# Attention, Fourier mixing and two feed-forward layers in one kernel: inputs handed over in the order of use, half the features in the first Fourier contraction, five probability buffers

## The chip, the core and the metric

The kernel runs on one core of a Trainium2 chip. TensorE (PE) multiplies matrices and transposes, VectorE (DVE) and ScalarE (ACT) do elementwise work, GpSimd (POOL) does elementwise work on SBUF alone and issues some DMAs, and SyncE (SP) issues most DMAs. Each engine takes its instructions in the order in which the program was written for it. PE writes to PSUM only, and DVE or ACT must carry its results on. The metric is the device time of one execution in microseconds (us); lower is better. What the host does with the inputs ahead of the launch is not in that time.

## The reference, cut to what matters

```python
# q, k, v: (4 batches, 8 heads, 576 rows, 64), float32
scores = (q @ k.T) / 8
scores = where(scores >= max(scores) - tau, scores, -1e9)
attn   = softmax(scores) @ v
x   = concat of the heads              # (4, 576, 512)
u   = x + real(fft(fft(x, axis=1), axis=2))
un  = (u - mean) / sqrt(var + 1e-6)    # over the 512 features
y   = u + relu(un @ w_ch1) @ w_ch2     # 512 -> 2048 -> 512
gate = sigmoid(causal 5-tap convolution of y over the rows, per feature)
out = (gate * (y @ w_val)) @ w_out
```

The weights come as float64 and are converted on the chip. Everything is kept at float32 accuracy: a matrix product with a weight or a Fourier table is three products of "high" and "low" parts (names end in h and l).

## The kernel before

The program has three stages, which follow one another on PE.

**Attention and Fourier mixing** (function attention_fft). The work goes by 16 pairs of heads, four pairs a batch. A pair has nine score tiles of 128 queries; two tiles make a unit, so there are 72 units. What each engine gets in a unit, and in which order, stands in one string (ORDER, line 34): each word is one step, T for the transposes of the probabilities of two units ago, S for the next scores, M, TH, E, K for maximum, threshold, exponential and masking, N for the division by the row sums. In order of data: PE makes scores s (line 582); DVE takes the maximum neg (594) and the threshold thr (597); ACT makes e (601); DVE masks into p and sums (611); POOL divides p by the sum (618); PE turns p into t (652); ACT copies it to m (661); PE multiplies m with v (318). The score tiles have two PSUM buffers, so the scores of the next unit wait until DVE has masked the tile before (line 611).

Between those fixed steps PE gets *filler* work in two places of each unit (P1 and P2, budgets of 1250 and 1350 ns), taken from queues in the order of QORD: the transposes of the last 64 keys (632), the preparation of the next pair's q and k, the Fourier products, the products with v. Steps on POOL, SP and ACT that belong to fillers run as *side* generators, advanced twice in a unit (A1, A2).

- Preparation of q and k (g_prep_qk, 247): natural q and k tiles are loaded in 128-partition pieces of 64 floats a row (load_qk, 179), q twice. PE turns them (258, 268, 277: 14 transposes a pair), DVE copies the keys out of PSUM (264, 272), ACT copies the queries and scales them by alpha = 1/8 (271, 279).
- Fold (g_fold, 331): a pair's x is stored to a DRAM tile xs; POOL makes sums and differences of row n and row 576-n (346, 348), ACT their high part (351), POOL the low part (355). All four pairs of a batch go into the contraction.
- Fourier products (g_fft, 376): stage one contracts the 512 features (four blocks of 128) with cosines and sines: 6 output blocks of 12 products, 72 a batch (line 398, recorded at 242). Stage two contracts rows: 45 products a batch (421). Features 257 to 511 are the mirror of 1 to 255, so the second half is fetched in reversed order (xr); the reversal goes through DRAM in two DMAs (turn_blocks 368, turn_order 372), and again for the result (472 to 481).

While this runs, weight pieces (40 in all) are loaded by POOL, converted on DVE, ACT and POOL (lines 96 to 106) in slots of the same units, and the first 18 are stored to DRAM and fetched back when room in SBUF comes free.

**Feed-forward** (mlp). Five chunks of columns; per chunk 16 steps of 12 products h (1083) and 12 products c (1099). Chunk 0 is interleaved with the last batch's Fourier products (line 1275), the rest follow.

**Gate and output** (gate_out): convolution on DVE, products v (1396) and o (1414).

## Time and profile before

| | |
|---|---|
| runs of the kernel before | 919.17 us median of 3 (919.12 to 919.69) |
| the profiled execution | 920.12 us, its span 918.3 us |
| PE busy | 874.0 us, 95% of the span |
| DVE, ACT, POOL busy | 558.9, 452.6, 370.1 us |
| granted PE clock, mean | 0.998 |
| DMA | 127.03 MB in 135019 packets, 87454 of them under 512 B |

A busy share is the union of an engine's instruction times. PE's matmuls overlap, so the mean duration of one (0.28 us for a transpose) is longer than the time from one to the next; for the pace one takes a run of several. The shares are averages over stages with different limits, so they are read stage by stage below.

### The profile page before, as it was taken

To read this page: it belongs to the slowest core of one execution; us is meant where nothing else is said; L and a number is where in the kernel's file an instruction comes from. 1 tells how busy PE (TensorE), PEld (TensorE's weight loads), DVE (VectorE), ACT (ScalarE), POOL (GpSimd) and SP (SyncE) were. 2 spreads that over 40 slices of the span, in tenths; PEclk is the share of its full clock that TensorE was granted. 3 is DMA by queue.
4 is the path that set the end of the run, shared out by engine and by line. 5 is a ranking of instruction groups with operands and counts; after the bars stand their busy time and mean duration, and the time that the engine had idled before them with its cause. 6 is when DMAs were issued, how large, how long until landed. Compare 5 with 4: busy or idle time off the path is not lost.

```text
span 918.3 us, 14887 instructions
## 1 busy us (share of the span) xinstructions
PE 874.0 (95%) x5232; PEld 693.7 (76%) x5232; DVE 558.9 (61%) x1240; ACT 452.6 (49%) x915; POOL 370.1 (40%) x451
## 2 busy tenths in 40 slices
PE   5988899999899999999999999999999999999998
PEld 3555576656656676578878999999888888898896
DVE  6888888888887676625885445434122375626740
ACT  4787777777776766735553333223112122214432
POOL 2465654675467427624563232221110201047421
PEclk9999999999999999999999999999999999999999
DMA  6776565567556622599259541421200230154101
GB/s 152 197 182 149 162 185 161 162 198 195 165 172 204 155 90 65 156 331 351 93 163 340 211 168 36 146 76 37 90 1 1 97 99 1 46 184 144 63 36 70
DMA packets 135019, 127.03 MB, mean 138 GB/s; under 512 B 87454, under 2 KB 93854, under 8 KB 134944
## 3 DMA queue, kind: packets, MB, share of 16 engines
q1 hardware_dynamic: 126496, 101.26, 36.0%
q0 software_dynamic: 6960, 24.49, 8.8%
q8 instruction: 42, 0.69, 0.3%
q10 hardware_dynamic: 1488, 0.33, 0.2%
q14 instruction: 33, 0.27, 0.1%
HBM read 93.53 MB, written 41.96 MB: 148 GB/s over the span
## 4 chain that ended last, share of the span: by engine, by line
PE 69%; DVE 12%; issue 9%; POOL 4%; ACT 4%; DMA 2%; SPq 0%; DVEq 0%; POOLq 0%; ACTq 0%
PE c L1099 16%; PE h L1083 16%; PE f L318 8%; PE s L582 7%; PE f L242 6%; PE o L1414 5%; PE v L1396 4%; PE t L652 4%; DVE p L611 4%; DVE neg L594 3%; ACT e L601 1%; PE f L632 1%; DVE ct L97 1%; POOL p L618 1%; PE f L277 1%
## 5 line engine op out<-in xcount | busy, mean ns | idle before, releaser
L1086 ACT ACTIVATE hh<-h 128x512 fp32r<-128x512 f32 (+1 forms) x80 | 44.3, 554 | 248.3 <-PE h L1083 248.2
L1087 DVE SCALAR_TENSOR_TENSOR hl<-h,hh 128x512 fp32r<-128x512 f32 (+1 forms) x80 | 50.8, 636 | 182.1 <-ACT hh L1086 182.1
L618 POOL TENSOR_SCALAR p<-p,su 128x576 f32<-128x576 f32 x144 | 110.6, 774 | 90.0 <-DVE su L708 70.8
L611 DVE SCALAR_TENSOR_TENSOR p<-s,thr,e 128x576 f32<-128x576 f32 x144 | 112.6, 815 | 39.9 <-ACT e L601 20.7
L582 PE MATMUL s<-kt,qt 64*128 64x288 f32 (+1 forms) x640 | 100.5, 445 | 24.7 <-DVE p L611 24.7
L1099 PE MATMUL c<-hl,w1h 128*128 128x512 f32 (+1 forms) x320 | 117.8, 368 | 0.4 <-DVE hl L1087 0.4
L1099 PE MATMUL c<-hh,w1h 128*128 128x512 f32 (+1 forms) x320 | 117.6, 367 | 0.0
L1099 PE MATMUL c<-hh,w1l 128*128 128x512 f32 (+1 forms) x320 | 117.5, 367 | 0.0
L594 DVE TENSOR_REDUCE neg<-s 128x1 f32<-128x576 f32 x144 | 101.5, 744 | 18.3 <-PE s L582 18.3
L601 ACT ACTIVATE e<-s,neg 128x576 f32<-128x576 f32 x144 | 99.5, 736 | 22.6 <-DVE neg L594 22.1
L582 PEld LDWEIGHTS s<-kt,qt 64*128 64x128 f32 (+1 forms) x640 | 45.7, 176 | 66.4 <-DVE p L611 22.8
L661 ACT ACTIVATE m<-t 128x512 f32<-128x512 f32 x144 | 84.6, 587 | 8.7 <-PE t L652 8.7
L318 PE MATMUL f<-m,v 128*64 128x320 f32 (+1 forms) x512 | 80.4, 415 | 1.6 <-ACT m L661 1.3
L652 PE MATMUL t<-ident,p 128*128 128x128 f32 x576 | 78.7, 279 | 2.3 <-POOL xf L346 1.2
L1083 PE MATMUL h<-unh,w0h 128*128 128x512 f32 (+1 forms) x320 | 79.1, 369 | 1.0 <-DMA w0h<-e_h 0.9
L1083 PE MATMUL h<-unh,w0l 128*128 128x512 f32 (+1 forms) x320 | 78.9, 368 | 0.1
L1083 PE MATMUL h<-unl,w0h 128*128 128x512 f32 (+1 forms) x320 | 78.7, 367 | 0.0
L652 PEld LDWEIGHTS t<-ident,p 128*128 128x128 f32 x576 | 64.2, 142 | 18.7 <-POOL p L618 8.4
L1099 PEld LDWEIGHTS c<-hl,w1h 128*128 128x128 f32 x320 | 60.1, 188 | 8.7 <-DVE hl L1087 1.2
L1083 PEld LDWEIGHTS h<-unh,w0h 128*128 128x128 f32 x320 | 58.5, 188 | 9.7 <-DMA w0h<-e_h 1.3
L1099 PEld LDWEIGHTS c<-hh,w1l 128*128 128x128 f32 x320 | 60.1, 188 | 7.2
L1099 PEld LDWEIGHTS c<-hh,w1h 128*128 128x128 f32 x320 | 60.1, 188 | 7.3
(219 smaller groups left out, 1543.5 us busy)
## 6 DMA issues: line engine op xcount, KB each, us to landing
raw<-in_moe_w_ch POOLq DMA_DIRECT2D x32, 512.0 KB, 5.0
qn<-in_q SPq DMA_DIRECT2D x60, 128.0 KB, 3.0
xs<-xt SPq DMA_DIRECT2D x16, 288.0 KB, 2.8
e_h<-cx SPq DMA_DIRECT2D x18, 256.0 KB, 4.4
e_l<-ct SPq DMA_DIRECT2D x18, 256.0 KB, 2.1
ypad<-y_d SPq DMA_DIRECT2D x16, 288.0 KB, 2.9
out<-os SPq DMA_DIRECT2D x18, 256.0 KB, 2.0
w0h<-e_h SPq DMA_DIRECT2D x17, 256.0 KB, 5.4
```

The costliest lines, as they stand in the source:

```text
L242: PE.matmul(out=o, lhsT=l, rhs=r, start=(i == 0), stop=(i == n - 1))
L318: PE.matmul(out=f[h * 64:h * 64 + 64, 0:n], lhsT=w, rhs=r, start=(t == 0), stop=(t == 4))
L582: PE.matmul(out=s[o, c, 0:HALF], lhsT=qt[w, hh, q], rhs=kt[w, hh, :], start=True, stop=True)
L594: DVE.tensor_reduce(out=neg[i][:, j, 0:1], in_=sc[g][:, :, 0:HALF], axis=AX.XY, op=ALU.max, negate=True)
L601: ACT.activation(e, sc[g][:, :, 0:HALF], AF.Exp, bias=neg[g // 2][:, g % 2, 0:1], scale=1.0)
L611: DVE.scalar_tensor_tensor(out=p_view(g).rearrange("p (a b) -> p a b", a=2), in0=sc.pop(g)[:, :, 0:HALF], scalar=thr[g // 2][:, j], in1=ex ...
L618: POOL.tensor_scalar(out=v, in0=v, scalar1=su, scalar2=1.0, op0=ALU.mult, op1=ALU.mult)
L652: PE.matmul(out=f[:, t, :], lhsT=pv[:, t * 128:(t + 1) * 128], rhs=ident, is_transpose=True, start=(t == 0), stop=(t == 3))
L661: tq.append(lambda: ACT.activation(o, fv, AF.Copy))
L1083: PE.matmul(out=f[:, 0:n], lhsT=ww[:, k * 128:(k + 1) * 128], rhs=x[:, k, 0:n], start=(i == 0), stop=(i == 3 * KB - 1))
L1087: DVE.scalar_tensor_tensor(out=hl, in0=f[:, 0:n], scalar=0.0, in1=f32(hh), op0=ALU.max, op1=ALU.subtract)
L1099: PE.matmul(out=ch[c][o][:, 0:n], lhsT=ww[:, o * 128:(o + 1) * 128], rhs=x, start=(at_ == 0 and i == 0), stop=(at_ == FB - 1 and i == 2))
```

## The change

The host now hands over q transposed (64 features by both heads' 576 rows), k transposed with its two halves on two sets of 64 partitions, v in tile order, all with the features of heads 4 to 7 mirrored, and the weights' rows and columns permuted to match. The kernel loads q and k where they are used; POOL scales k by alpha (DVE for the first pair). The pairs are taken in the order 2, 3, 0, 1: the upper two are only stored (reversed order comes by itself) and read back as *mirror*; for the lower two POOL adds and subtracts the mirror (1152 columns more) before the fold. Stage one contracts two feature blocks instead of four, plus one small product `od` that carries the alternating term of feature 256. The result's second half is stored without a reversal. PBUFS goes from 4 to 5. The marks that open room for the feed-forward stage are set by unit (LEFT = 100, in tiles), and the last chunk uses its weight slots from the highest down.

```diff
-PBUFS = 4
+PBUFS = 5
+WAIT_QK = 2
+LEFT = 100
-QORD = (1, 0, 4, 2, 3)
+QORD = (0, 3, 1, 2)
+PAIRS = (2, 3, 0, 1)
+TURN = (2, 2)
...
+            kt = qk_p.tile([128, 2, HALF], F32, tag="kt", name="kt")
+            qt = qk_p.tile([128, 2, S], F32, tag="qt", name="qt")
+            SP.dma_start(out=kt, in_=a["k"][b, n])
+            for j, q in enumerate((SP, second)):
+                q.dma_start(out=qt[j * 64:j * 64 + 64], in_=a["q"][b, n])
+            return qt, kt
+
+        def g_prep_qk(p):
+            qt, kt = load_qk(p)
+            for _ in range(WAIT_QK):
+                yield
+            POOL.tensor_scalar(out=kt, in0=kt, scalar1=alpha[:, 0:1], scalar2=1.0, op0=ALU.mult, op1=ALU.mult)
+            kq[p] = (qt, kt)
...
-                    PE.transpose(f[:, o:o + 128], kn[:, j, h].rearrange("p g d -> p (g d)"), ident)
...
-                done(lambda: None, lambda: DVE.tensor_copy(kt[:, :, 0:256], fk))
...
-                PE.transpose(f[:, h * 96:h * 96 + 96], tn[:, h].rearrange("p g d -> p (g d)"), ident[0:96, 0:96])
...
-                    PE.transpose(f[:, t * 128:(t + 1) * 128], qn[:, h, t].rearrange("p g d -> p (g d)"), ident)
...
-                done(lambda f=f, h=h: ACT.activation(qt[:, h, 0:MAIN], f, AF.Identity, scale=alpha[:, 0:1]))
...
+            if j >= 2:
+                r = 1 + 128 * (3 - j)
+                SP.dma_start(out=rev[r:r + 128], in_=x)
+                if j == 2:
+                    SP.dma_start(out=rev[0:1], in_=x[127:128])
+                folded.add(p)
+                if p % NP == 1:
+                    for _ in range(TURN[0]):
+                        yield
+                    while b and b - 1 not in spent_fold:
+                        yield
+                    ms = [fft_p.tile([128, S], F32, tag=f"mirror{i}", name="mirror") for i in range(2)]
+                    for i, m in enumerate(ms):
+                        SP.dma_start(out=m, in_=rev[i * 128:(i + 1) * 128])
...
+            eng = DVE if p == NPAIR - 1 else POOL
...
+            eng.tensor_tensor(out=d, in0=x, in1=m, op=ALU.subtract)
+            yield
+            eng.tensor_tensor(out=m, in0=x, in1=m, op=ALU.add)
+            yield
+            turn(1, d, ALU.subtract)
+            if j == 0:
+                POOL.tensor_tensor(out=t[1][0:1, inner], in0=d[0:1, inner], in1=d[0:1, back], op=ALU.add)
+            yield
+            turn(0, m, ALU.add)
+            high_part(1)
+            yield
+            low_part(1)
             high_part(0)
             yield
-            high_part(1)
             low_part(0)
...
-                    for xx, dd in ((xh, dh), (xl, dh), (xh, dl)):
-                        for j in range(NP):
-                            yield mm(f[0:m, 0:n], xx[:, j, n0:n0 + m], dd[:, j, 0:n], i, 12)
-                            i += 1
+                    terms = [(xx[:, j, n0:n0 + m], dd[:, j, 0:n]) for xx, dd in ((xh, dh), (xl, dh), (xh, dl)) for j in range(2)]
+                    if kind == 0:
+                        terms += [(xx[:, 0, n0:n0 + m], cst["od"]) for xx in fold[b][1]]
+                    for i, (xx, dd) in enumerate(terms):
+                        yield mm(f[0:m, 0:n], xx, dd, i, len(terms))
...
-            turn_blocks(blocks, rev, 16)
-            if j == 0:
-                SP.dma_start(out=u_d[b][256:257], in_=rev[0:1])
-            yield
-            turn_order(u_d[b][DM - 127 - 128 * j:DM + 1 - 128 * j], blocks, 16)
+            SP.dma_start(out=u_d[b][DM // 2 + 128 * j:DM // 2 + 128 * j + 128], in_=xr)
```

On PE, at the start of the program, before the change (kn, tn, qn are natural keys, tails and queries; s the scores):

```order
L258 MATMUL f<-ident,kn 128x128 x4
L268 MATMUL f<-ident,tn 128x96 x2
L277 MATMUL f<-ident,qn 128x128 x8
L582 MATMUL s<-kt,qt 128x288 x4
L258 MATMUL f<-ident,kn 128x128 x4
L268 MATMUL f<-ident,tn 128x96 x2
L582 MATMUL s<-kt,qt 128x288 x4
L277 MATMUL f<-ident,qn 128x128 x8
```

The same place after the change, down to the first products with v:

```order
L539 MATMUL s<-kt,qt 128x288 x12
L609 MATMUL t<-ident,p 128x128 x8
L539 MATMUL s<-kt,qt 128x288 x4
L609 MATMUL t<-ident,p 128x128 x8
L589 MATMUL f<-ident,p 64x128 x4
L539 MATMUL s<-kt,qt 64x288 x4
```

All transposes of q and k are gone; the first three units (four products s each) have nothing on PE but scores.

On PE, the cosine part of stage one of the first batch before (cdh, cdl are the table's parts, xeh, xel the folded sums):

```order
L242 MATMUL f<-cdh,xeh 97x258 x4
L242 MATMUL f<-cdh,xel 97x258 x3
L652 MATMUL t<-ident,p 128x128 x8
L242 MATMUL f<-cdh,xel 97x258
L242 MATMUL f<-cdl,xeh 97x258 x4
```

and after:

```order
L231 MATMUL f<-cdh,xeh 97x258 x2
L231 MATMUL f<-cdh,xel 97x258 x2
L231 MATMUL f<-cdl,xeh 97x258 x2
L231 MATMUL f<-od,xoh 97x258
L231 MATMUL f<-od,xol 97x258
```

Twelve products became eight; a sine block goes from twelve to six.

On POOL, the fold of one pair and the divisions around it before (xt is the pair's x, xf and xel parts of the fold):

```order
L346 TENSOR_TENSOR xf<-xt 128x287
L348 COPY xf<-xt 128x2
L618 TENSOR_SCALAR p<-p,su 128x576
L346 TENSOR_TENSOR xf<-xt 128x287
L618 TENSOR_SCALAR p<-p,su 128x576
L355 TENSOR_TENSOR xel<-xf,xeh 128x289
```

and after, for a lower pair, with a weight piece's step (ct, raw) and the scaling of the next keys (kt):

```order
L330 TENSOR_TENSOR diff<-xt,mirror 128x576
L575 TENSOR_SCALAR p<-p,su 128x576
L332 TENSOR_TENSOR mirror<-xt,mirror 128x576
L575 TENSOR_SCALAR p<-p,su 128x576
L320 TENSOR_TENSOR xf<-diff 128x287
L321 COPY xf<-diff 128x2
L575 TENSOR_SCALAR p<-p,su 128x576
L109 TENSOR_TENSOR ct<-raw 128x512
L841 DMA raw<-in_moe_w_ch 128x1024
L320 TENSOR_TENSOR xf<-mirror 128x287
L321 COPY xf<-mirror 128x2
L194 TENSOR_SCALAR kt<-kt,alpha 128x576
```

The divisions that PE waits for now stand behind operations of 576 columns and behind the scaling of the keys, which itself waits for a load.

## Rows read from the trace of the kernel before

**Rows 1.** Windows: stretch, length, busy time of each engine, clock, DMA.
```profile
core 0: us, PE busy (x) PEld busy (x) DVE busy (x) ACT busy (x) POOL busy (x), PEclk, DMA share, GB/s
9.54:380.33 370.79, 342.40 (x2484) 226.76 (x2485) 297.83 (x732) 270.00 (x573) 211.47 (x283) 1.00 0.59 163
9.54:120.00 110.46, 95.50 (x672) 59.70 (x672) 94.85 (x236) 83.78 (x175) 63.49 (x87) 0.98 0.70 178
120.00:300.00 180.00, 169.81 (x1245) 115.09 (x1244) 146.64 (x358) 133.49 (x285) 109.92 (x145) 1.00 0.62 177
300.00:380.00 80.00, 76.76 (x572) 51.77 (x567) 56.04 (x139) 52.40 (x116) 37.73 (x52) 1.00 0.39 110
380.00:394.00 14.00, 11.49 (x86) 6.75 (x82) 6.68 (x11) 9.14 (x20) 11.05 (x15) 1.00 0.60 195
394.00:498.00 104.00, 101.44 (x495) 84.29 (x494) 68.10 (x107) 51.57 (x97) 44.52 (x49) 1.00 0.71 247
498.00:812.30 314.30, 313.86 (x1565) 282.25 (x1564) 131.80 (x243) 82.83 (x144) 55.25 (x52) 1.00 0.26 87
812.30:918.30 106.00, 101.40 (x601) 91.22 (x599) 50.11 (x124) 36.88 (x78) 47.15 (x48) 1.00 0.27 95
```
**Rows 2.** Line 597: the thresholds; duration least, median, most in ns; first, last start.
```profile
L597 DVE TENSOR_REDUCE thr<-neg x72: 142/157/158, 12.6 to 380.3; 128x2 f32<-128x4 f32 x72
```
**Rows 3.** Timeline of a unit near 218 us: start, duration, idle before and releaser.
```profile
215.28 1.09 PE L277 MATMUL f<-ident,qn 128*128 128x128 f32 x8
...
218.97 0.81 DVE L611 SCALAR_TENSOR_TENSOR p<-s,thr,e 128x576 f32<-128x576 f32 x1
...
219.49 1.24 PE L582 MATMUL s<-kt,qt 64*128 64x288 f32 x8
...
219.71 1.32 DVE L97 TENSOR_SCALAR ct<-raw 128x512 int32<-128x512 int32 x1
```
**Rows 4.** Groups by line and form: busy us, mean ns, idle before, releasers.
```profile
L264 DVE COPY kt<-f 128x512 f32<-128x512 f32 x16 | 10.9, 684 | 1.6 <-PE f L258 1.6
...
L618 POOL TENSOR_SCALAR p<-p,su 128x576 f32<-128x576 f32 x144 | 110.6, 774 | 90.0 <-DVE su L708 70.8 <-PE s L582 12.3 <-PE f L277 4.6
...
L346 POOL TENSOR_TENSOR xf<-xt 128x287 f32<-128x287 f32 x32 | 26.5, 827 | 6.9 <-ACT xt L321 6.8
...
L1341 POOL TENSOR_TENSOR y1l<-ypad,y1h 128x576 fp32r<-128x576 f32 x4 | 5.6, 1432 | 0.0
...
L97 DVE TENSOR_SCALAR ct<-raw 128x512 int32<-128x512 int32 x40 | 27.9, 709 | 0.0
```
**Rows 5.** The keys' second copy from 9.54 to 120; a conversion step's least, median, most.
```profile
L272 DVE COPY kt<-f 128x64 f32<-128x64 f32 x6 | 1.3, 215 | 0.5 <-ACT qt L271 0.3
...
L97 DVE TENSOR_SCALAR ct<-raw x40: 409/423/2637, 40.1 to 596.7; 128x512 int32<-128x512 int32 x40
```
**Rows 6.** The chain that ended last, in order of time: start, duration, what.
```profile
1.66 4.16 DMA kn<-in_k
...
9.54 2.25 PE s L582 x8
...
128.06 2.34 PE f L242 x18
```
**Rows 7.** DMA issues by line: count, KB each, us to landing (median).
```profile
xs<-xt SPq DMA_DIRECT2D x16, 288.0 KB, 2.8
...
xr<-xr SPq DMA_DIRECT2D x7, 288.0 KB, 8.0
```
**Rows 8.** Who waited for whom, 9.54 to 394: us, times, longest.
```profile
PEld t L652 <- POOL p L618: 8.4, 15, 1.4
...
POOL xd L460 <- DMA xd<-xs: 4.8, 1, 4.8
```
**Rows 9.** Windows around the drop of the clock at the start.
```profile
12.67:19.80 7.13, 3.89 (x25) 2.25 (x25) 5.58 (x17) 3.86 (x8) 4.24 (x6) 1.00 0.66 144
19.80:23.20 3.40, 3.24 (x14) 2.11 (x14) 2.96 (x7) 1.97 (x3) 1.46 (x2) 0.50 1.07 339
```

More of the change, by code (lines that the diff above doesn't have):

```diff
@@ L328, in attention_fft @@
         folded, spent_fold, added = set(), set(), set()
-        xs_d = {}
+        xs_d, rev_d, mirror = {}, {}, {}
         def g_fold(p):
-            b, j = p // NP, p % NP
+            b, j = p // NP, PAIRS[p % NP]
             x = xt.pop(p)
-            while p and p - 1 not in folded or b and b - 1 not in spent_fold:
+            while p and p - 1 not in folded:
+                yield
+            if p % NP == 0:
+                xs_d[b] = dram.tile([DM // 2, S], F32, name=f"xs{b}")
+                rev_d[b] = dram.tile([DM // 2 + 1, S], F32, name=f"xr{b}")
+            xs, rev = xs_d[b], rev_d[b]
+            if j >= 2:
[12 more added lines that the diff above has]
+                        SP.dma_start(out=m, in_=rev[i * 128:(i + 1) * 128])
+                    for _ in range(TURN[1]):
+                        yield
+                    for i, m in enumerate(ms):
+                        mirror[b, i] = m
+                return
+            SP.dma_start(out=xs[j * 128:(j + 1) * 128], in_=x)
+            while (b, j) not in mirror or b and b - 1 not in spent_fold:
@@ new lines, in g_fold, with turn @@
+            m = mirror[b, j]
+            d = fft_p.tile([128, S], F32, tag="diff", name="diff")
+            t = [tmp_p.tile([128, KE], F32, tag="xf", name="xf") for _ in range(2)]
+            ends, inner, back = slice(0, HALF + 1, HALF), slice(1, HALF), slice(S - 1, HALF, -1)
+            eng = DVE if p == NPAIR - 1 else POOL
+            def turn(kind, s, op):
+                POOL.tensor_tensor(out=t[kind][:, inner], in0=s[:, inner], in1=s[:, back], op=op)
+                POOL.tensor_copy(t[kind][:, ends], s[:, ends])
@@ L350, in high_part @@
             def high_part(kind):
-                ACT.activation(fold[b][kind][0][:, j, w[kind]], xf[kind][:, w[kind]], AF.Copy)
+                ACT.activation(fold[b][kind][0][:, j, 0:HALF + 1], t[kind][:, 0:HALF + 1], AF.Copy)
             def low_part(kind):
-                h, l = (t[:, j, w[kind]] for t in fold[b][kind])
-                POOL.tensor_tensor(out=l, in0=xf[kind][:, w[kind]], in1=f32(h), op=ALU.subtract)
-            sums(0)
+                h, l = (q[:, j, 0:HALF + 1] for q in fold[b][kind])
@@ L385, in g_fft @@
             for kind in range(2):
-                if kind:
-                    turn_order(rev[1:257], blocks, 16)
                 xh, xl = fold[b][kind]
@@ L769, in attention_fft @@
             hooks["tick"]()
-            if left and NPAIR - 1 in kq:
-                left.close()
-                left = None
+            if t == LEFT:
                 yield "left"
@@ L1281, in mlp @@
             last = c == NCH - 1
-            js = sorted(range(FB), key=lambda j: slots.index(slot_of[j]) < FB - FIRST) if last else range(FB)
+            js = sorted(range(FB), key=lambda j: -slots.index(slot_of[j])) if last else range(FB)
             for n, j in enumerate(js):
@@ L1541, in shape_constants, with laid_out @@
     return {k_: np.ascontiguousarray(v, dtype=np.float32) for k_, v in c.items()}
+def laid_out(a):
+    heads = [*range(H // 2)] + [p ^ 1 for p in range(H // 2, H)]
+    q, k, v = (a[n][:, heads].copy() for n in "qkv")
+    v[:, H // 2:] = v[:, H // 2:, :, ::-1]
+    q, k, v = (x.reshape(B, NP, 2, S, D) for x in (q, k, v))
+    c = {"q": q.transpose(0, 1, 4, 2, 3).reshape(B, NP, D, 2, S)}
+    c["k"] = k.reshape(B, NP, 2, 2, HALF, D).transpose(0, 1, 3, 5, 2, 4).reshape(B, NP, 2 * D, 2, HALF)
+    c["v"] = v[:, :, :, :MAIN].reshape(B, NP, 2, MAIN // 128, 128, D).transpose(0, 1, 4, 2, 3, 5).reshape(B, NP, 128, 2, MAIN // 128, D)
+    c["vt"] = v[:, :, :, MAIN:].transpose(0, 1, 3, 2, 4).reshape(B, NP, TAIL, 2, D)
+    f = [*range(DM // 2 + 1)] + [*range(DM - 1, DM // 2, -1)]
+    c["moe_w_ch1"], c["moe2_w_out"] = a["moe_w_ch1"][f], a["moe2_w_out"][f]
+    c["moe_w_ch2"], c["moe2_conv_w"] = a["moe_w_ch2"][:, f], a["moe2_conv_w"][:, f]
+    c["moe2_w_val"] = a["moe2_w_val"][f][:, f]
+    return {n: np.ascontiguousarray(x) for n, x in c.items()}
 _INS = ["q", "k", "v", "tau", "moe_w_ch1", "moe_w_ch2", "moe2_w_val", "moe2_conv_w", "moe2_w_out"]
@@ L1554 @@
     arrays["tau"] = np.reshape(arrays["tau"], (1,))
+    arrays.update(laid_out(arrays))
     arrays.update(shape_constants())
```

139 lines of the change are left out of this document (29 added, 110 removed).

## The prediction

> **What bounds the kernel now.** I read the windows by stage first, then the timeline of one unit, the groups by line and form, and last the waits. The windows [rows 1] show three regimes. From 498 to 918.3 us PE is busy 313.86 of 314.30 and 101.40 of 106.00 us, with products that the change leaves as they are: nothing is to be had there. From 394 to 498 it is busy 101.44 of 104.00 us, with chunk 0 and the last batch's Fourier products. The attention stage, from the first score at 9.54 us to the last threshold, takes 370.8 us; PE is busy 342.4 of them (92%), DVE 297.8 (80%), and the balance moves: up to 120 us the two are level (95.50 and 94.85 of 110.46), up to 300 us PE leads (169.81 to 146.64 of 180), and up to 380 us by far (76.76 to 56.04 of 80).
>
> A unit takes (380.3 - 12.6) / 71 = 5.18 us [rows 2]. Its timeline shows why neither engine gets to 100% [rows 3]: eight score instructions (each product is two) take 1.24 us on PE after DVE's mask, and DVE, which cannot take the next maximum without them, does a conversion step meanwhile. A unit is as long as the longer of two loads: PE's steps and fillers in order, or DVE's. Less filler shortens only units in which PE is the longer.
>
> **What goes from PE and DVE.** Eight transposes take 1.09 us with the drain of the last one in it [rows 3], so about 0.12 us from one to the next; 14 a pair are 1.6 us. Stage one goes from 72 products a batch to 42 (three cosine blocks of 8, three sine blocks of 6) at 2.34 / 18 = 0.13 us [rows 6]: 3.9 us a batch. DVE loses two key copies a pair, 0.684 [rows 4] and 0.215 us [rows 5], 0.9 us together. ACT's copies and scalings of q go as well; ACT leads in no stretch [rows 1], so I book nothing for them.
>
> By stretch, with PE and DVE of [rows 1]:
> - 9.54 to 120 us: six pairs' preparation (the second key copy counts six [rows 5]). PE 95.5 - 9.8 = 85.7, DVE 94.9 - 5.4 = 89.5 us: DVE is now the longer. Level engines reached 86.5% here; at 88% the stretch takes 101.7 us, 8 less (7 at 86.5%).
> - 120 to 300 us: seven pairs and two batches' stage one. PE 169.8 - 11.5 - 7.8 = 150.5, DVE 146.6 - 6.3 = 140.3. DVE stands at 93% of PE, where it was 86% and PE reached 94%; between that and the first stretch I take 91%: 165.4 us, 14.6 less.
> - 300 to 380 us: two pairs and one batch. PE 76.8 - 3.3 - 3.9 = 69.6, DVE 54.2. PE stays the longer, at 95%: 73.2 us, 6.8 less.
>
> Together 29.4 us. The bounds: 36 us if every microsecond taken from PE counts (15 pairs by 1.6 and three batches by 3.9), 13.5 us if only DVE's copies count.
>
> **What is added.** POOL gets 15 scalings of k (576 columns, like the division's 0.774 us) and 14 additions or subtractions of 576 columns with two operands (1.432 us, like y1l) [rows 4]: 11.6 + 20.0 us. The rest of the fold is done for two pairs instead of four, about seven operations like xf, 0.827 us [rows 4], fewer a batch, which pays some 20 us of that back; POOL's total rises by some 12 us on 211.5 [rows 1] and it stays far from full. What counts is order: behind them wait the divisions, and behind those PE's transposes, which have waited 8.4 us for POOL so far [rows 8]. A division stands idle for 90.0 / 144 = 0.63 us before it starts [rows 4], which covers most of a scaling. Uncovered are 15 by 0.15 and 14 by 0.8 us, 13.5 us in all; since a division is made a unit ahead of its transpose, I take 2.5 (0 to 13.5).
>
> The scaling of k also waits for a load that is issued one unit, about 5 us, ahead. Loads of 288 KB landed after 2.8 us (median), the worst kind after 8.0 [rows 7]. Queued behind the waiting scaling are the two divisions of that unit, and PE behind them. I take nothing: the load is ahead by more than the median. The dearer end is the third rival.
>
> On conversions: a step of line 97 takes 423 ns in the median, 709 in the mean and 2637 at most [rows 4, 5], on operands of one size, so something holds DVE up. The Trainium skill (SBUF — State Buffer, "Who interferes with whom") says that DVE and GpSimd share a port pair, and that one of them blocks for the other's whole instruction when DVE copies or scales in a two-port mode or has two SBUF inputs; the trace agrees with it, 2637 ns against 423. By that rule more and longer POOL work lengthens the conversions, which speaks against the change.
>
> **Start.** The first load landed 4.16 us after it began at 1.66 us [rows 6], and then came transposes and copies until the first scores at 9.54. Now a load of 288 KB and one scaling on DVE (0.41 to 0.68 us [rows 4, 5]) come first: 1.66 + 4.16 + 0.5 = 6.3 us, 3 us sooner (4.5 with the 2.8 us landing; 0.7 later than now with 8.0). I take 3.
>
> But the clock: from 12.67 to 19.80 us PE was busy 3.89 of 7.13 us, and behind that the granted clock fell to 0.50 for 3.4 us, the 1.2 GHz level; from there on it stood at full [rows 9]. Now the first three units hold scores alone, so the lower level lasts longer. Eight score instructions at half the clock cost 1.24 us more a unit [rows 3]: I take 1.5 us (0 to 3.7 for three units). The Trainium skill (TensorE: Matmul & The Clock Gate, "The HAM clock gate") calls the throttled state the default that activity releases; the trace agrees, with 0.50 behind the thin stretch.
>
> **End of the attention stage.** From 380 to 394 us POOL is the busiest engine (11.05 of 14 us, PE 11.49 with gaps [rows 1]). Now the last divisions stand beside two operations of 1.432 us where two of 0.827 stood [rows 4]: 1.5 us later (0 to 2.9). **Chunk 0**: the last batch's 30 products fewer are 3.9 us of a stage in which PE is at 97.5%; DVE (68.1 us) and the weights' arrival give some back: 3.5 (1 to 4.5).
>
> The fifth probability buffer, the order of weight slots in the last chunk, and the reversal through DRAM that goes change nothing that PE waits for in [rows 8] for long: 0.
>
> **Sum.** -29.4 + 2.5 - 3 + 1.5 + 1.5 - 3.5 = -30.4 us on the profiled 920.1 us (span 918.3 and 1.8 around it), 889.7. That execution lies 0.95 us above the median 919.17, so 888.8; I say 888, since ACT's relief is not booked. What is late next is DVE in the first 120 us and PE still afterwards.
>
> **Rivals.**
> First, PE is the longer in every unit after all: conversions are moved by their own queue into PE's time, and all of 36 us counts, with 3.9 from chunk 0, 4.5 at the start and no cost on POOL or in the clock: 920.1 - 44.4 - 0.95 = 875. For it: PE leads for two thirds of the stage. Against: the level shares of the first stretch.
>
> Second, POOL's new work shows in full: 13.5 us instead of 2.5 where divisions stand behind it, or the same through DVE's held conversions. 888 + 11 = 899. For it: 2637 ns in line 97. Against: a lead of one unit.
>
> Third, slower: the scaling of k waits on POOL for its load in every pair. The longest wait of POOL for a load so far is 4.8 us [rows 8]; less the idle time ahead of two divisions (1.25 us) that is 3.55 us by 15 pairs, 53 us: 941. It decides from 31 / 15 = 2.1 us a pair. Against: SP issues it a unit ahead, and the small packets that filled the DMA queues go.
>
> Fourth, the fillers only filled time that PE spent waiting for DVE. Then only start and chunk 0 are left, at their low ends, against the costs on POOL and in the clock: no change, about 919. Against: after 120 us DVE is idle for a fifth of the time and more.
>
> **Chances.** Forecast 0.61 (878 to 896 by itself), first rival 0.18, second 0.13, third 0.05, fourth 0.03. The range 868 to 903 holds the forecast with most of the first two. Below 0.2% (1.8 us) this kernel's runs cannot tell from no change. Faster by more: 0.61 + 0.18 + 0.13 = 0.92; same 0.03; slower 0.05.
>
> **What would show it.** The first score near 6.3 us. The last threshold near 352 us, units of 4.8 us. In a window over the first 100 us, DVE busier than PE; later PE near 91%. PE's waits for the division (8.4 us now) up by two or three us; in the tens they would mean the second rival. POOL waiting for the load of kt for tens of us would mean the third. From the end of chunk 0 to the last output, 420 us as now; if that stretch moves by more than 2 us, the sum misses a term.

## The result, and the profile after

The changed kernel takes 907.63 us (median of 4 runs, 907.4 to 910.67), beside 919.43 for the kernel before on the same chip: a ratio of 0.988, with a 95% interval of 0.9865 to 0.9895. It is faster, as forecast, but by 12 us instead of 31, and 907.6 lies outside the range of 868 to 903. The profiled execution took 907.40 us, its span 905.6.

The windows of the kernel after, by the stages of [rows 1] (stretch, length, busy time of each engine, clock, DMA):

```profile
core 0: us, PE busy (x) PEld busy (x) DVE busy (x) ACT busy (x) POOL busy (x), PEclk, DMA share, GB/s
8.01:367.95 359.94, 316.91 (x2192) 199.49 (x2193) 298.57 (x702) 243.36 (x511) 222.97 (x284) 0.97 0.52 157
...
368.00:381.80 13.80, 9.41 (x73) 5.87 (x71) 5.66 (x10) 8.97 (x20) 11.36 (x13) 1.00 0.61 197
381.80:486.00 104.20, 99.25 (x467) 82.76 (x466) 70.44 (x110) 52.21 (x97) 45.48 (x50) 0.98 0.68 240
486.00:799.50 313.50, 313.35 (x1562) 281.87 (x1561) 130.50 (x242) 82.84 (x144) 55.29 (x52) 1.00 0.24 81
799.50:905.60 106.10, 101.33 (x601) 91.16 (x599) 50.10 (x124) 36.87 (x78) 47.14 (x48) 1.00 0.21 77
```

Against [rows 1], the first score comes 1.5 us sooner, the attention stage loses 10.8 us (370.8 to 359.9), the end of that stage and chunk 0 lose nothing (13.7 to 13.8, 104.0 to 104.2), and the rest 0.7: together the 12.7 us between the two spans. In the stage PE's busy time fell by 25.5 us, where some 36 us of work went, and the lower granted clock, 0.97 instead of 1.00, accounts for the rest: 316.9 by 0.97 is 307. And PE's idle time in the stage rose from 28.4 to 43.0 us. DVE's busy time did not fall (297.8 to 298.6), although 13.5 us of key copies went. The waits in and just behind the stage, 8.01 to 382, say where PE stood (us in all, times, longest):

```profile
PEld t L609 <- POOL p L575: 26.9, 30, 2.4
PE s L539 <- DVE p L568: 26.4, 26, 2.1
POOL kt L194 <- DMA kt<-in_k: 22.7, 5, 9.4
...
PE t L609 <- POOL p L575: 15.2, 16, 2.0
...
POOL cs L954 <- DMA z<-u_d: 1.6, 1, 1.6
```

PE's weight loads for the transposes waited 8.4 us for POOL's division [rows 8]; now 26.9 (in the stage alone 7.0 and 24.4). (PE's own wait lies in part beside that of its weight loads, so the two rows are not added.) The place to look is POOL. Its groups in the stage, to be read beside [rows 4] (busy, mean ns, idle before, releasers):

```profile
L575 POOL TENSOR_SCALAR p<-p,su 128x576 f32<-128x576 f32 x141 | 109.7, 784 | 57.7 <-DVE su L661 56.4 <-PE t L609 0.5
...
L194 POOL TENSOR_SCALAR kt<-kt,alpha 128x576 f32<-128x576 f32 x15 | 11.2, 744 | 33.1 <-DMA kt<-in_k 22.7 <-DVE su L661 4.7 <-PE s L539 4.3
...
L330 POOL TENSOR_TENSOR diff<-xt,mirror 128x576 f32<-128x576 f32 x6 | 8.4, 1408 | 4.5 <-ACT xt L270 4.5
L332 POOL TENSOR_TENSOR mirror<-xt,mirror 128x576 f32<-128x576 f32 x6 | 8.4, 1405 | 0.1
```

The sizes are as forecast. What was not: POOL's idle time ahead of a division fell from 90.0 to 57.7 us, that is, a division found POOL taken where it used to find it waiting. Two units show how. The first is near 74 us (start, duration, idle before and releaser):

```profile
73.78 0.73 POOL L194 TENSOR_SCALAR kt<-kt,alpha 128x576 f32<-128x576 f32 x1 [4.18 <-DMA kt<-in_k]
...
74.51 3.45 POOL L575 TENSOR_SCALAR p<-p,su 128x576 f32<-128x576 f32 x4
75.30 0.42 PEld L609 LDWEIGHTS t<-ident,p 128*128 128x128 f32 x4 [2.45 <-POOL p L575]
```

POOL waited 4.18 us for the load of kt; four divisions had piled up behind it, and PE's transposes waited 2 us. The second is the longest unit of all, from the threshold at 267.79 to that at 279.43, 11.6 us where a unit has 5:

```profile
269.98 2.77 POOL L954 TENSOR_TENSOR cs<-z 128x512 f32<-128x512 f32 x2 [1.58 <-DMA z<-u_d]
...
270.13 1.50 DVE L105 TENSOR_SCALAR raw<-cx 128x512 int32<-128x512 int32 x1
...
271.55 1.75 DVE L103 SCALAR_TENSOR_TENSOR cx<-raw,cx 128x512 int32<-128x512 int32 x1
...
272.74 1.18 POOL L575 TENSOR_SCALAR p<-p,su 128x576 f32<-128x576 f32 x1
...
273.97 0.42 PEld L609 LDWEIGHTS t<-ident,p 128*128 128x128 f32 x4 [1.87 <-POOL p L575]
...
274.54 1.25 POOL L956 TENSOR_TENSOR cs<-cs 128x512 f32<-128x512 f32 x1
...
275.82 0.63 ACT L934 ACTIVATE cs<-cs 128x512 fp32r<-128x512 f32 x1 [4.97 <-POOL cs L956]
...
276.49 1.58 DVE L935 TENSOR_TENSOR cs<-cs 128x512 fp32r<-128x512 f32 x1 [3.10 <-ACT cs L934]
276.57 0.66 PE L609 MATMUL t<-ident,p 128*128 128x128 f32 x4 [1.94 <-POOL p L575]
```

Here the earlier mark (LEFT = 100) put the column sums of chunk 0's z on POOL in the middle of the attention stage. All four engines wait, one behind the other: POOL for a DMA, ACT and PE for POOL, DVE for ACT. Two conversion steps of DVE (105 and 103) take 1.50 and 1.75 us beside POOL's two column sums, where their medians in the stage are 0.42 and 0.69. My forecast did not price this part of the change at all.

### The profile page after: what moved, and what is told of

Its sections match the earlier page's. It is cut to its first block, busy times and chain, and to the rows that moved or that the text cites. A ratio compares the mean times of both kernels' runs of the same rounds, so it can differ in the third digit from the quotient of the medians.

```text
span 905.6 us, 13922 instructions
## 1 busy us (share of the span) xinstructions
PE 840.3 (93%) x4888; PEld 661.2 (73%) x4888; DVE 559.6 (62%) x1211; ACT 425.8 (47%) x851; POOL 382.4 (42%) x451
## 4 chain that ended last, share of the span: by engine, by line
PE 60%; DVE 9%; issue 8%; POOL 5%; DMA 2%; ACT 2%; SPq 0%; DVEq 0%; POOLq 0%; ACTq 0%
PE c L1050 17%; PE h L1034 17%; PE o L1365 5%; PE f L267 5%; PE v L1347 4%; PE s L539 4%; PE f L231 4%; PE t L609 3%; DVE p L568 2%; DVE neg L551 1%; DMA z<-u_d 1%; DVE ct L100 1%; POOL p L575 1%; POOL res L1059 1%; DVE cx L103 1%
## 5 line engine op out<-in xcount | busy, mean ns | idle before, releaser
L539 PE MATMUL s<-kt,qt 64*128 64x288 f32 (+1 forms) x640 | 104.7, 459 | 37.0 <-DVE p L568 26.4
L575 POOL TENSOR_SCALAR p<-p,su 128x576 f32<-128x576 f32 x144 | 112.4, 786 | 57.7 <-DVE su L661 56.4
L551 DVE TENSOR_REDUCE neg<-s 128x1 f32<-128x576 f32 x144 | 101.7, 744 | 17.4 <-PE s L539 17.2
L539 PEld LDWEIGHTS s<-kt,qt 64*128 64x128 f32 (+1 forms) x640 | 50.4, 185 | 79.6 <-issue 45.0
L609 PE MATMUL t<-ident,p 128*128 128x128 f32 x576 | 85.6, 290 | 16.8 <-POOL p L575 15.2
L609 PEld LDWEIGHTS t<-ident,p 128*128 128x128 f32 x576 | 65.5, 146 | 47.0 <-POOL p L575 26.9
L267 PE MATMUL f<-m,v 128*64 128x320 f32 (+1 forms) x512 | 74.2, 421 | 1.4 <-ACT m L618 1.4
L1034 PEld LDWEIGHTS h<-unl,w0h 128*128 128x128 f32 x320 | 59.3, 190 | 7.7
```

The lines of the kernel that those rows point to most:

```text
L267: PE.matmul(out=f[h * 64:h * 64 + 64, 0:n], lhsT=w, rhs=r, start=(t == 0), stop=(t == 4))
L539: PE.matmul(out=s[o, c, 0:HALF], lhsT=qt[w, hh, q], rhs=kt[w, hh, :], start=True, stop=True)
L551: DVE.tensor_reduce(out=neg[i][:, j, 0:1], in_=sc[g][:, :, 0:HALF], axis=AX.XY, op=ALU.max, negate=True)
L575: POOL.tensor_scalar(out=v, in0=v, scalar1=su, scalar2=1.0, op0=ALU.mult, op1=ALU.mult)
L609: PE.matmul(out=f[:, t, :], lhsT=pv[:, t * 128:(t + 1) * 128], rhs=ident, is_transpose=True, start=(t == 0), stop=(t == 3))
L1034: PE.matmul(out=f[:, 0:n], lhsT=ww[:, k * 128:(k + 1) * 128], rhs=x[:, k, 0:n], start=(i == 0), stop=(i == 3 * KB - 1))
```

## The experiments

Theory Q: what the change took from PE was given back because POOL, in program order, now stands ahead of PE with side work (scalings, mirror operations, column sums). Rivals: D, DVE's work sets the unit; P, PE's does; C, the lower clock by itself. The table has every run with its ratio to the kernel before (95% interval), and from its profile the first score, the stage from there to the last threshold, PE's and DVE's busy time in it and the mean granted clock of the stage.

| run | ratio | first score | stage | PE, DVE | clock |
|---|---|---|---|---|---|
| before | 1 | 9.5 | 370.8 | 342, 298 | 1.00 |
| after | 0.988 (.9865-.9895) | 8.0 | 359.9 | 317, 299 | 0.97 |
| no_pool | 0.974 (.9723-.9757) | 6.6 | 349.8 | 312, 293 | 0.99 |
| wait5 | 0.9839 (.982-.9858) | 6.8 | 358.5 | 316, 297 | 0.97 |
| mirror_dve | 0.984 (.9823-.9857) | 6.8 | 357.0 | 315, 302 | 0.97 |
| left130 | 0.9839 (.9815-.9863) | 8.6 | 355.3 | 313, 295 | 0.98 |
| combo | 0.978 (.9761-.9799) | 8.9 | 353.4 | 315, 301 | 0.97 |
| pbufs4 | 1.0018 (1.0009-1.0028) | 8.8 | 374.7 | 323, 297 | 0.95 |
| before_p5 | 0.994 (.9925-.9954) | 9.5 | 365.9 | 340, 298 | 1.00 |
| p6 | 0.9863 (.9848-.9878) | 8.5 | 357.9 | 313, 298 | 0.99 |
| fft72 | 0.9938 (.9921-.9955) | 8.7 | 366.2 | 327, 294 | 0.97 |
| before_fft42 | 0.9965 (.9949-.9981) | 9.4 | 366.8 | 334, 302 | 0.99 |
| nopool_fft72 | 0.9733 (.9712-.9754) | 7.0 | 349.4 | 318, 288 | 1.00 |
| before_kact | 1.0003 (.9991-1.0014) | 9.2 | 370.9 | 340, 290 | 1.00 |
| nopool_dve | 0.9814 (.9791-.9836) | 8.2 | 355.5 | 314, 302 | 0.98 |
| start | 0.9849 (.9834-.9864) | 4.9 | 362.3 | 318, 299 | 0.97 |
| mean1 | 0.9855 (.9829-.9882) | 8.6 | 359.8 | 314, 297 | 0.97 |
| combo_p6 | 0.9751 (.9736-.9766) | 4.9 | 352.9 | 315, 300 | 0.97 |
| best_act | 0.9703 (.9678-.9729) | 4.9 | 347.7 | 311, 299 | 0.99 |
| best_cw | 0.9684 (.9651-.9717) | 4.8 | 350.4 | 313, 301 | 0.98 |

### What POOL's additions cost

**no_pool** leaves all of POOL's additions out of the computation (the scalings of kt, the differences and sums with the mirror); PE's instructions keep their order word for word.

```diff
-            POOL.tensor_scalar(out=kt, in0=kt, scalar1=alpha[:, 0:1], scalar2=1.0, op0=ALU.mult, op1=ALU.mult)
...
-            eng.tensor_tensor(out=d, in0=x, in1=m, op=ALU.subtract)
+            d = x
...
-            eng.tensor_tensor(out=m, in0=x, in1=m, op=ALU.add)
```

> Leaves out of the computation what the change added on POOL: the scaling of kt for pairs 1 to 15 and the difference and sum with the mirror (x and the mirror are folded as they are). 11.2 + 16.8 us of POOL's work in attention and its 22.7 us of waits for kt go; PE's, ACT's and DVE's work stays. Theory Q: PE's waits for p fall from 42 us to 10 to 20, the clock rises, time 889 to 898, near my forecast of 888. Rival D: 904 to 908, since DVE's 299 us in 360 stay. Rival C: 904 to 908.

The ratio falls by 0.014, 12.9 us: Q's number, not D's or C's. In the profiles the stage is 10.1 us shorter, and the first score, which the edit does not touch, came 1.4 us sooner. The run takes three things away at once: POOL's work ahead of the divisions, the waits for kt's load, and what POOL's work does to DVE's conversions (last part). The waits for the division fall (window of the stage, where the changed kernel has 24.4 and 13.7; line 572 is the division here), though not to what they were before (7.0 and 1.0):

```profile
PEld t L606 <- POOL p L572: 15.3, 21, 2.2
PE t L606 <- POOL p L572: 6.9, 7, 1.9
```

**wait5, mirror_dve, left130**: the three hold-ups one by one.

```diff
-WAIT_QK = 2
+WAIT_QK = 5
```


> One number changed: the scaling of a pair's kt comes 5 side steps behind its load's issue instead of 2 (some 2.5 units instead of 1). In the changed kernel POOL stood 22.7 us in 5 waits for these loads (longest 9.4), with the divisions of p queued behind. Theory Q (POOL's queue in program order is what TensorE now waits for): the waits go, PE's waits for p fall from 42 us by 8 to 15, time 901 to 905. Rival D (VectorE's work per unit sets the pace, POOL's waits lie beside it): 907 to 908. Rival C (the lower granted clock of thin stretches is the cause by itself): the clock stays near 0.97 and the time at 907.

```diff
-            eng = DVE if p == NPAIR - 1 else POOL
+            eng = DVE
```


> The 12 difference and sum operations that ran on POOL (1.41 us each, 16.8 us) run on DVE, as the last pair's already do, some 0.7 us each by DVE's mask of the same size, 8 to 9 us in sum. Theory Q: POOL gains more than DVE loses, time 902 to 906. Rival D: DVE's 8 to 9 us show, time 911 to 916.

```diff
-LEFT = 100
+LEFT = 130
```


> One number changed: the place at which the MLP's first buffers are taken, chunk 0's z is loaded and its column sums are made, from unit 50 to unit 65. Theory Q in its part Z: the unit of 11.65 us at 268 to 279, in which POOL waits for z and adds 4 us, goes back to some 5 us, and the clock of 265 to 300 rises from 0.85: time 901 to 905. Rival: the same hold-up comes 15 units later, or ahead of chunk 0, time 906 to 910.

Each is 0.4% faster than the changed kernel, by intervals that do not overlap its own (they were timed beside other runs of the kernel before). The profiles separate them better. In wait5 no wait for kt's load is left, but the stage is only 1.4 us shorter, and the first score, which the edit does not touch, came 1.2 us sooner in that profile. By the ratios the edit is worth 3.8 us (0.0041); the one profile and the medians agree no better. Either way the 22.7 us of the most visible wait were worth little; that POOL catches up behind it (four divisions in a row at 74.51) is my reading of one unit. mirror_dve shortens the stage by 3.0 us although DVE's busy time rises by 4. left130 shortens it by 4.6, of which the stretch behind it takes 2.7 back (13.9 to 16.6 us from the last threshold to the first h): a part of the column sums' price seems to have moved there, as the rival had it.

**combo**: the three together.

> The three single edits together: kt scaled 5 side steps behind its load, the 12 mirror operations on DVE, chunk 0's buffers taken at unit 65. Each alone gave 0.4% against the changed kernel. Theory Q (each takes away a different hold-up of the divisions): the gains add, 12 us and some less for what the leave-out of POOL's added work gave in all (1.4%), ratio to the kernel before 0.973 to 0.978 against 0.988 of the changed kernel. Rival (they are three ways to take away the same wait, or the wait only moves on): 0.982 to 0.985.

0.978, a full per cent below the changed kernel. The three single gains make 0.0122 in all, so they add for the most part, as Q said. PEld's wait for the division is 10.8 us in its stage.

### What the fifth buffer was worth

**pbufs4** (the changed kernel with PBUFS = 4), **before_p5** (the kernel before with 5; mlp_h is taken at the mark "rows" instead of "scores"), **p6** (the changed kernel with 6).

> Four probability buffers instead of five, all else as changed. I had booked the fifth at nothing; in the kernel before DVE waited 10.7 us for a buffer of p to be read (27 waits or so, none long). Theory Q: with POOL's divisions late, the fifth buffer is what lets DVE go on, so its loss costs 2 to 5 us, 910 to 913. Rival (a buffer is never what ends last): 907 to 908.

> The kernel before with one part of the change alone: five probability buffers instead of four (to find the room, the MLP's buffers for h are taken some units later, when the probabilities' are given back). In the kernel before DVE waited 10.7 us for a buffer, and the planner, which holds a mask back until its buffer's tail is transposed, pulled filler forward there. Theory F (the buffer is worth as much without the rest: nearly all of the gain is its own): 906 to 912. Theory G (it is worth something only where the divisions are late, as in the changed kernel, where its loss cost 14 us): 915 to 920. My forecast booked nothing: 919.

> The changed kernel with six probability buffers, in the same order of instructions on every engine, so only waits for a free buffer go. Theory F: with five DVE still waits for a buffer in the long units, 1 to 4 us less, 904 to 907. Rival (five are enough; what made four dear was the order that the planner is forced into): 907 to 908.

With four buffers the change is no gain at all: 1.0018, and the stage, 374.7 us, is longer than before. That is far more than the 2 to 5 us that I expected. Its waits name a place (8.81 to 383.48):

```profile
POOL kt L194 <- DMA kt<-in_k: 33.6, 8, 10.2
DVE p L568 <- PE f L589: 26.0, 12, 4.1
PEld t L609 <- POOL p L575: 25.2, 32, 2.2
```

A buffer comes free when PE has transposed its tail (589), that comes behind the division, and the division is late; so DVE's mask waits 26.0 us for a buffer, and with it the loop. With five there is no such wait. But the program also moves work when the buffer count changes: a mask is held back until its buffer's tail is transposed, and filler is pulled forward until then. By the traces PE's instructions stand in another order in 36 places in pbufs4 (POOL's are in the same order), and in 43 in before_p5. How much of the price is the wait and how much that order, no run separates. In the kernel before, where divisions are early, the setting gains 0.6% (5.5 us): 914.4, between theory F's 906 to 912 and G's 915 to 920, and not the nothing that I booked. The sixth, with every engine's order unchanged, gains nothing that can be told from the changed kernel (0.9863 beside 0.988, with overlapping intervals).

### Whether PE's or DVE's work set the unit

**fft72** makes the first 4 or 6 products of each block twice in the changed kernel, so 30 a batch are back; **nopool_fft72** does the same in no_pool; **before_fft42** leaves 30 a batch out of the kernel before.

```diff
+                    for i in range(12 - len(terms)):
+                        yield mm(f[0:m, 0:n], *terms[i], i, 12 - len(terms))
                     for i, (xx, dd) in enumerate(terms):
                         yield mm(f[0:m, 0:n], xx, dd, i, len(terms))
```

> The changed kernel with stage one of the Fourier transform at 72 products a batch again: the first 4 (cosine) or 6 (sine) products of each block are made twice, so nothing else moves than PE's work, 0.13 us each, 3.9 us a batch. Theory P (PE's filler work counts in full, as my sum had it): 15 to 17 us more, 922 to 925, or 11 to 13 where chunk 0 hides the last batch. Theory Q (in the changed kernel TensorE has slack, since divisions and DVE end last in many units): 4 to 8 us more, 911 to 915.

> The kernel before with 42 products a batch in stage one instead of 72 (the other 30 are left out of the computation): nothing else changes but PE's work, 3.9 us a batch, 15.6 us in all. My sum's shares for what is taken from PE: 12 to 13 us less, 906 to 908. Theory S (the kernel before already had units in which DVE was the longer, so PE's filler counted for two fifths there too, as the 72 products put back into the changed kernel did): 4 to 8 us less, 911 to 915.

> Leaves out of the computation what the change added on POOL, as an earlier run did (ratio 0.974), and makes stage one's products 72 a batch again. Theory Q (POOL's hold-ups make the slack in which PE's work hides): here PE's work counts in full, 12 to 16 us more than without, ratio 0.987 to 0.991. Theory S (the slack is DVE's units, with or without POOL): 4 to 8 us more, 0.978 to 0.983.

The 15.6 us of products count for 5.3 us in the changed kernel (0.0058), 3.2 in the kernel before, and nothing without POOL's additions (0.9733 beside 0.974). P falls, and so does Q's part that PE's work would count in full once POOL is out of the way (S's 0.978 to 0.983 is missed too). Against what I expected, these runs do not move PE's amount of work alone: the filler budgets then cut the queue elsewhere, and the traces show PE's instructions in another order in 54 places (61 in before_fft42), and DVE's, ACT's and POOL's too. So the prices are those of the products with the order that they bring. The windows of no_pool and of nopool_fft72 over the stage show a part of it:

```profile
6.64:356.41 349.77, 311.59 (x2192) 195.60 (x2193) 292.71 (x706) 243.14 (x511) 195.05 (x258) 0.99 0.54 162
```
```profile
6.98:356.39 349.41, 317.88 (x2282) 204.64 (x2283) 287.79 (x702) 241.82 (x511) 192.95 (x257) 1.00 0.55 163
```

90 more products, 11.7 us at the 0.13 of [rows 6], raise PE's busy time by 6.3 us only, beside a clock that rises from 0.99 to 1.00. The Trainium skill (TensorE: Matmul & The Clock Gate, "The HAM clock gate") calls the throttled state the default that activity releases; these two rows agree with that. It is not general: in the changed kernel the same 90 products (fft72) left the stage's clock at 0.97 and raised PE's busy time by 10.4 us.

**before_kact** (KEYS_ACT = 1) moves the larger key copy from DVE to ACT in the kernel before; **nopool_dve** puts both copies on DVE again in no_pool:

```diff
+            if i == 1 and h < 2:
+                w = 256 if h == 0 else 32
+                DVE.tensor_copy(extra[:, :, 0:w], sc[g][:, :, 0:w])
```

> The kernel before with the larger key copy of each pair (0.684 us) on ACT instead of DVE; PE's and POOL's order stays word for word. DVE loses 16 by 0.684 = 10.9 us. Theory D (DVE's loop of maximum, threshold, mask and conversions sets the unit in the kernel before, and that PE was 92% busy only says that its filler fits beside it): 8 to 12 us less, 908 to 912. Theory P (PE sets it): 917 to 920. Between: both in turn, 4 us less.

> Leaves out of the computation what the change added on POOL, as an earlier run did (ratio 0.974), and gives DVE two copies a pair again, of the sizes of the key copies that the change removed (512 and 64 columns out of PSUM, into a buffer that nobody reads). Theory D: DVE's 15 by 0.9 us show, ratio 0.985 to 0.989. Theory P: 0.974 to 0.977.

Neither theory holds in both. Neither edit changes PE's order. 10.9 us less on DVE gain nothing before (1.0003; DVE's busy time fell by 8 us, the stage stayed at 370.9). But the copies went to ACT, and DVE now waits there. Before, then before_kact, in the stage:

```profile
DVE p L611 <- ACT e L601: 20.7, 27, 1.5
```
```profile
DVE p L611 <- ACT e L601: 24.0, 28, 1.5
DVE kt L272 <- ACT qt L271: 6.0, 14, 1.4
```

The wait for qt was 0.3 before, so 9 us of new waits for ACT stand against the 10.9: the run shows what moving the copy is worth, not what dropping it would be. In nopool_dve 14.6 us of copies (32 of them, right ahead of masks) cost 6.8 (0.0074), between D's and P's numbers. So PE's 15.6 us were worth 3.2 in the kernel before, and DVE's copies stay unpriced there. A cut that takes from both is what no run here separates; the 14 transposes a pair were not put back alone, ACT's relief neither, and the cuts were not made together in the kernel before. What stays open is this: without POOL's additions the stage is 21 us shorter than before, and the single prices that were measured (5.0 for the buffer and 4.0 for the products, by the stages of before_p5 and before_fft42, and 5.8 for the copies by that of nopool_dve) make 14.8 of it, if they add.

### The start and chunk 0

**start** loads pair 0's q in two parts, 128 columns first; **mean1** puts one more turn between chunk 1's column sums and their product on PE.

```diff
+            parts = (slice(0, S),) if p else (slice(0, 128), slice(128, S))
+            for c in parts:
                 for j, q in enumerate((SP, second)):
-                    q.dma_start(out=qt[j * 64:j * 64 + 64], in_=a["q"][b, n])
+                    q.dma_start(out=qt[j * 64:j * 64 + 64, :, c], in_=a["q"][b, n][:, :, c])
```


> Pair 0's q is loaded in two parts: first the 128 columns that the first scores need (64 KB for each half of the partitions), then the other 448. In the changed kernel the first score waited for 288 KB a half, landed at 8.0 us, while kt was scaled by 5.97. Theory B (bytes in the queues ahead of it set the first score): first score at 6.0 to 6.6 us, time less by 1 to 2 us, 905.5 to 906.5. Rival (the first units wait for something else anyhow, or the lower clock of a thin start eats it): 907 to 908.

```diff
             yield
+            if c == 1:
+                yield
             mu = col_mean(parts)
```


> The mean of chunk 1's columns comes one turn later in the cycle of chunk 0. In the changed kernel its product on TensorE waited 3.9 us for cs, which stood behind two pieces of conversion on DVE, with the h and c products queued behind it. Theory M (this wait is where chunk 0's 3.5 us went): the wait goes, chunk 0 takes 100 to 101.5 us instead of 104.2, time 904 to 905.5. Rival (DVE's conversions set the end of chunk 0's second part anyhow, or chunk 1's centring comes too late): 907 to 909.

start brings the first score from 8.0 to 4.86 us (timeline of PE), so the bytes ahead of it did set it:

```profile
4.86 3.35 PE L541 MATMUL s<-kt,qt 64*128 64x288 f32 x8 [4.86 <-DVE atau L632]
```

but those eight products take 3.35 us, the next come late, and the stage is 2.3 us longer; 0.8 us are left in the profile, and some 0.3% by the ratios (0.9849 beside 0.988, their intervals just apart): less than theory B's 1 to 2 us in the first, 2.9 us in the second. In chunk 0 (381.8 to 486 of the changed kernel, then 381 to 486 of mean1) the wait only changed its name:

```profile
PEld mean L945 <- DVE cs L935: 3.9, 1, 3.9
```
```profile
PEld c L1052 <- DVE hl L1040: 4.2, 2, 2.7
```

First h to first v took 418.5 us with it, 417.6 without, and the ratio (0.9855) cannot be told from the changed kernel's: the rival's number holds. That DVE's conversions of the last weights, in order ahead of both, set that part of chunk 0 is what the two waits suggest; no run takes the conversions out.

### A version that beats both

**combo_p6**: combo with start and six buffers; **best_act**: that with kt scaled by ACT; **best_cw**: that with the convolution weights converted 10 side steps behind their load instead of 4 (21.6 us instead of 10.4 in the traces).

```diff
-            POOL.tensor_scalar(out=kt, in0=kt, scalar1=alpha[:, 0:1], scalar2=1.0, op0=ALU.mult, op1=ALU.mult)
+            ACT.activation(kt, kt, AF.Copy, scale=alpha[:, 0:1])
...
             conv_w.load()
-            for _ in range(4):
+            for _ in range(10):
```

> All edits that helped together: kt scaled later, mirror operations on DVE, chunk 0's buffers at unit 65, pair 0's q in two parts, and six probability buffers. Theory Q with the start: ratio to before 0.974 to 0.977 where the three edits without the last two had 0.978. Rival (the start's gain and the sixth buffer are eaten by what is late next, DVE): 0.977 to 0.979.

> As the best version so far (kt scaled later, mirror operations on DVE, chunk 0's buffers at unit 65, q of pair 0 in two parts, six buffers; ratio 0.9751), with the scaling of kt on ACT instead of POOL, 15 times some 0.74 us. Theory Q (POOL's order still holds divisions up by these): ratio 0.972 to 0.974. Rival (kt's scaling lies in POOL's idle time once its load has come): 0.975 to 0.977, the exponentials being held up instead.

> As the best version so far (ratio 0.9703), with three units between the load of the convolution's weights and their conversion instead of one; DVE waited 3 to 4 us for that load in each profile of the changed kernel. Theory D: the wait goes from DVE's path, 2 to 4 us less, 0.966 to 0.969. Rival (the unit was long anyhow): 0.970 to 0.971.

best_act, 892.96 us, is 3% faster than the kernel before and, by the ratios, 1.8% faster than the changed one; the last edit cannot be told from it. In its stage (4.88 to 352.62) everything that the change added is still computed, and PE waits less for the division than in no_pool:

```profile
4.88:352.62 347.74, 311.29 (x2192) 195.77 (x2193) 299.12 (x728) 251.03 (x526) 199.09 (x258) 0.99 0.56 163
```
```profile
PEld t L611 <- POOL p L577: 11.0, 19, 1.4
PE t L611 <- POOL p L577: 3.1, 4, 1.2
```

DVE is as busy there as in the changed kernel (299.1 beside 298.6 us), and the stage is 12.2 us shorter. So neither the amount of the added work nor DVE's total cost this, but on which engine and in which order the work stood. That best_act passes no_pool is no proof by itself, for it has the later mark, the split load and the sixth buffer besides. And the wait for the division is not the whole price of POOL's order: from combo_p6 to best_act PE's and DVE's orders stay, 11 us of scalings leave POOL, the ratio falls by 0.0048 and the stage by 5.2 us, while PEld's wait for the division goes from 9.6 to 11.0. What that last step shortened is open.

## Why the prediction was wrong, point by point

- **POOL's order, the step that failed first.** "Since a division is made a unit ahead of its transpose, I take 2.5 (0 to 13.5)." Measured: 12.9 us by the ratios, 10.1 in the stage (no_pool beside the changed kernel; the waits for kt's load and DVE's held conversions are in it), near the far end of the bound. In the two units shown a wait or two long operations held up two to four divisions, and PE waited for the first of them; the lead of a unit did not cover that. Rival 2 named this and its sign, PE's waits for the division in the tens, was there. Its 899 was still too low, because it kept the other terms of the sum.
- **The wait of kt's load.** "I take nothing: the load is ahead by more than the median." Five of 15 waited, 22.7 us in all, longest 9.4. The median (3.2 us, near the forecast's 2.8) says nothing on the loads that land late. But the price was far below rival 3's 53: the stage lost 1.4 us when these waits went, 3.8 by the ratios.
- **What goes from PE and DVE, -29.4 us.** Without POOL's additions the stage is 21 us shorter, so 8 us of this term fail even then, and more, for the fifth buffer's gain, booked at 0, is in the 21. The share was mis-sized at its source: I took PE's filler to count by PE's busy share, and products taken from it alone counted for 3.2 of 15.6 us. A busy share of 92% was not a limit of 92%; this is close to the fourth rival, to which I gave 0.03. (The sum has a slip besides: 89.5 us at 88% is 101.7, which is 8.8 less than 110.5 and not 8.) One sign held: from 8 to 120 us DVE is now the busier, 95.2 us to PE's 91.9.
- **DVE's copies, 13.5 us of it.** They did not lower DVE's busy time: the five conversion steps, of unchanged number and size, took 53.1 us in the stage before and 63.7 after. One of them, before and after (the 709 of [rows 4] is over the whole run before):

```profile
L97 DVE TENSOR_SCALAR ct<-raw 128x512 int32<-128x512 int32 x18 | 10.3, 575 | 0.0
```
```profile
L100 DVE TENSOR_SCALAR ct<-raw 128x512 int32<-128x512 int32 x18 | 12.8, 709 | 0.0
```

  With POOL's additions out, and DVE's order otherwise the same, the five took 57.6 us (no_pool), and with the products at 72 they went from 58.7 (fft72) to 52.4 (nopool_fft72): POOL's additions lengthened them by 6 us, and what came with fewer products by 5. The 90 steps of a stage fall into two kinds: those with no POOL operation beside them have a mean of 538 ns before, 517 after and 521 in no_pool; those that overlap one have 658 (40 of them), 875 (48) and 796 (39). (A longer step meets a POOL operation more easily, so the split alone proves little; the run without POOL's additions does not depend on it.) The rule on the shared port that the prediction cited (the Trainium skill, SBUF — State Buffer, "Who interferes with whom") would have it so by POOL's longer work; these means agree with it. The prediction named this effect and put no term into the sum for it; why fewer products go with longer conversions stays open.
- **The clock, +1.5 (0 to 3.7).** The first units kept theirs (1.00 from 8 to 60 us); it fell later, to 0.96 from 60 to 215 us, and lowest around the long unit shown above:

```profile
265.00:300.00 35.00, 27.05 (x161) 15.33 (x161) 26.48 (x57) 17.95 (x39) 27.61 (x34) 0.85 0.47 152
```

  Over the stage 0.97 by 316.9 us of PE's time are some 9 us of PE's; how many of them are on the path no run shows.
- **The fifth buffer: 0.** 5.5 us alone, and within the change 12.7 by the ratios of pbufs4 and the changed kernel (0.0138 of 920), 14.4 by their medians, with the order that the setting brings. I looked for it among PE's waits [rows 8]; it was DVE that waited for a buffer, in the loop of maximum, exponential and mask. The kernel before, 9.54 to 394:

```profile
DVE p L611 <- PE f L632: 10.7, 6, 2.7
```

- **The start, -3.** -1.5. The model was right, the load's time was off: 288 KB of q landed at 8.0 us, issued behind k and beside the next pair's loads, not after 4.16. Over the profiles the first score came between 6.6 and 8.9 us with these loads in this order.
- **Chunk 0, -3.5.** Nothing. PE's busy time there fell by 2.2 us (101.4 to 99.3, at a clock of 0.98 instead of 1.00), and its idle time rose by 2.4. mean1 points at DVE; the cause stays open.
- **The end of the stage, +1.5.** +0.1. **The rest**: 419.6 us against 420.3, as forecast.
- **Not in the sum**: the earlier mark, worth 4.6 us of the stage by left130. The diff showed it, and no term was made of it.

In the profiles the parts close: the stage 21.0 us shorter without POOL's additions, 10.1 longer again with them, 1.5 won at the start, 0.7 in the rest, and 0.3 lost at the end of the stage and in chunk 0, together 12.8, against 12.7 between the two spans.

## What to carry to other kernels

A busy share does not say what work taken away is worth; putting the same work in or out of a kernel does, and here it said one fifth in the kernel before and one third in the changed one. Work moved onto an engine with spare time is priced by what stands behind it in that engine's order, and an added wait by how many of the instructions behind it pile up; the cover of "one unit ahead" is spent by the first long operation. When a change adds a buffer beside other edits, price the buffer with the other edits in: it was worth 5.5 us alone and some 13 where the producer had become late. A trial that moves work to another engine prices the move, and not the work: look for the waits that came with it. Compare the order of instructions, too, before a run counts as a change in amount alone.

## What the runs showed of the hardware

- The granted clock of the stage did not go by how long PE was busy in all: 1.00 at 342 us (before), 0.95 at 323 (pbufs4), 1.00 at 318 (nopool_fft72). In the changed kernel it was lowest, 0.85, in the 35 us around the unit of 11.6 us; with that unit's column sums moved away (left130), the same 35 us had 0.95.
- The same conversion step on DVE, of one size, had stage means of 575, 709 and 531 ns in before, after and nopool_fft72. Over all five steps the mean without a POOL operation beside them stayed between 517 and 543 ns in the 15 profiles in which it was taken; with one it went from 656 to 875.
